# Expert stage of a fused attention and expert kernel: float32r mask, shared V tile for two batches' last tokens, outputs cut at query 256

## Chip, cores and metric

One Trainium2 chip; the kernel runs on 1 core. The metric is the device time of one execution in microseconds, taken as the median over several runs. Before the change it was run 3 times.

## The reference

Three blocks follow each other on 4 batches of 576 tokens, with 512 model columns. First comes an attention with 8 heads whose masks are local (4 heads) or strided (4 heads). Then a mixing layer with cosines, sines and token matrices. Then the block that the change is in, four causal attention experts with a gate that keeps two of them for each token:

```python
def _moe2_ref(x, w_gate, wq, wk, wv, wo):
    logits = x @ w_gate
    topk = np.argpartition(-logits, K, axis=-1)[..., :K]
    ...
    for e in range(E):
        q = x @ wq[e]
        k = x @ wk[e]
        v = x @ wv[e]
        scores = scale * (q @ k.transpose(0, 2, 1))
        scores = np.where(causal, -1000000000.0, scores)
        ...
        ye = a @ v @ wo[e]
        for kk in range(K):
            mask = topk[:, :, kk] == e
            out += mask[..., None] * w[:, :, kk:kk + 1] * ye
```

## The kernel before

Products keep nearly full float32 precision by splitting both sides into a high part in float32r and a low part (the rest). `mm3` (lines 252 to 255) is one such product in three matmuls: high by high, high by low, low by high.

The first 361 us are the sparse attention and the mixing layer; the change leaves their instructions as they are, but for one cast to bf16 at the start (line 73). Behind them the expert stage works batch by batch:

- `project_v` makes V and the gate's logits of a batch: five tiles of tokens, four of 128 and a last one of 64 (`TW`), each with 4 chunks of the model columns by 3 matmuls of 260 columns (256 of V, 4 of the gate). ScalarE casts the result to the high part (line 452), VectorE subtracts to the low part (line 453) and copies the logits (line 454). After the last tile `gates` works out the two best experts with some twenty small VectorE operations.
- `project_qk` makes Q and K of two experts in blocks of 288 tokens (12 matmuls each).
- `attention(b, e, ...)` runs 16 times (4 batches, 4 experts). For each tile t of queries it makes scores against all earlier keys in two matmuls (lines 533, 534), and a third adds the causal mask to the diagonal block: an identity in bf16 is the stationary side, the mask in bf16 the moving one (line 536). The last tile has 64 queries and 576 keys in two chunks of 288, the mask on 64 columns of the second. VectorE takes the maximum, ScalarE the exponential, GpSimd (VectorE for t = 0) scales, TensorE transposes (line 559), ScalarE casts to the high part `pthi` (line 567), VectorE makes the low part `ptlo` (line 568).
- After the loop over t the values are summed in two parts of 288 queries (lines 569 to 589). Key chunk c takes two matmuls, one on `ptlo` (line 579) and one on `pthi` (line 583). The first part has the column counts 288, 160, 32, the second 288, 288, 288, 192, 64, each twice. The result `o` has one PSUM buffer; ScalarE copies half of it (line 588), VectorE adds (line 589).
- `experts` splits the sums of two experts on GpSimd (lines 602, 603) and `output` multiplies by `wo` for one block of 128 model columns (m) and one part of the queries (n): 6 matmuls, a ScalarE copy into a staging slot in X[0] (line 615), and a DMA from SyncE's queue (line 616). There are four slots.

Tiles are recorded in program order and a scheduler that works with a timeline of its own sets the order on each engine; each engine then takes its instructions strictly in that order, and waits on semaphores. The `fill` lists hand projections and outputs of the neighbouring batches to the places in the attention loop from which they may be taken.

## Time and profile before

| what | value |
|---|---|
| median of 3 runs | 582.23 us (581.08 to 583.97) |
| profiled execution, its own time | 579.94 us |
| its span, first to last instruction | 578.2 us |
| TensorE matmul busy | 542.3 us, 94% of the span, 4560 matmuls |
| TensorE weight loads busy | 508.1 us, 88% |
| VectorE busy | 412.3 us, 71% |
| ScalarE busy | 316.2 us, 55% |
| GpSimd busy | 234.3 us, 41% |
| mean granted TensorE clock | 0.968 of full speed |

A busy TensorE here means that one matmul at least is in the pipeline. Matmuls overlap: one of 288 columns is shown as about 0.29 us long, but the next starts 0.13 us later. What a matmul costs is therefore read from the distance between two starts, not from its length.

### The profile page before, as it was taken

How to read it: one execution, taken by the hardware profiler on the slowest of the kernel's cores; microseconds unless marked ns; L12 is line 12 of the kernel's file. 1: busy time of each engine (PE TensorE's matmuls, PEld its weight loads, DVE VectorE, ACT ScalarE, POOL GpSimd, SP SyncE). 2: the span in 40 equal slices, each digit the busy share in tenths (PEclk: the TensorE clock that was granted, in tenths of full speed). 3: DMA queues.
4: the chain of work that ended last, by engine and by line, in shares of the span. 5: the costliest groups of instructions: out<-in, count | busy, mean ns of one | idle time of the engine just before them, and what ended most of it. 6: DMA issues, size and time to landing. Idle time of an engine off the chain costs nothing.

```text
span 578.2 us, 12507 instructions
## 1 busy us (share of the span) xinstructions
PE 542.3 (94%) x4560; PEld 508.1 (88%) x4560; DVE 412.3 (71%) x1205; ACT 316.2 (55%) x882; POOL 234.3 (41%) x314
## 2 busy tenths in 40 slices
PE   6787689899999999999999999899999999999996
PEld 6677579799999999999999999898989899899985
DVE  4896897995687456776255553488987888879882
ACT  5754966533536217254142550287678667866873
POOL 3532383650145211445104460365364534534452
PEclk9957969899999999999999999999999999999999
DMA  9557634221322013110100010100001001100012
GB/s 306 191 166 226 224 123 133 95 69 64 95 86 85 2 32 126 37 38 2 56 1 1 1 57 0 37 2 2 1 12 43 31 1 43 34 9 12 32 42 82
DMA packets 18660, 37.53 MB, mean 65 GB/s; under 512 B 2200, under 2 KB 9544, under 8 KB 18600
## 3 DMA queue, kind: packets, MB, share of 16 engines
q1 hardware_dynamic: 18600, 36.74, 19.6%
q8 instruction: 36, 0.59, 0.4%
q14 instruction: 24, 0.20, 0.1%
HBM read 32.01 MB, written 4.72 MB: 64 GB/s over the span
## 4 chain that ended last, share of the span: by engine, by line
PE 67%; DVE 14%; ACT 9%; DMA 5%; issue 2%; POOL 2%; SPq 0%; ACTq 0%; POOLq 0%; DVEq 0%
PE y L253 6%; PE y L254 6%; PE y L255 6%; PE tp L559 3%; PE th L253 3%; PE th L255 3%; PE th L254 3%; PE g L253 2%; PE g L254 2%; PE s L180 2%; PE g L255 2%; PE pq L253 2%; PE o L583 2%; PE s L533 2%; PE av L231 2%
## 5 line engine op out<-in xcount | busy, mean ns | idle before, releaser
L253 PE MATMUL y<-wtk_hi,zhi 128*128 128x288 f32 x288 | 86.9, 303 | 1.6 <-DVE cs L277 0.6
L254 PE MATMUL y<-wtk_lo,zhi 128*128 128x288 f32 x288 | 85.6, 298 | 1.0 <-POOL wtk_lo L100 1.0
L255 PE MATMUL y<-wtk_hi,zlo 128*128 128x288 f32 x288 | 84.5, 296 | 0.0
L314 POOL TENSOR_TENSOR zlo<-cs,zhi 128x512 fp32r<-128x512 f32 (+1 forms) x40 | 49.5, 1249 | 66.0 <-DVE zhi L311 42.1
L556 POOL TENSOR_SCALAR p<-p,sm,gt 128x256 f32<-128x256 f32 (+1 forms) x64 | 45.2, 709 | 57.2 <-DVE sm L554 38.9
L205 POOL TENSOR_TENSOR p<-p,sm 128x288 f32<-128x288 f32 (+2 forms) x48 | 32.3, 682 | 81.0 <-DVE sm L204 60.1
L549 ACT ACTIVATE p<-s,nm 128x128 f32<-128x128 f32 (+2 forms) x96 | 49.5, 517 | 14.8 <-DVE nm L538 10.0
L253 PEld LDWEIGHTS y<-wtk_hi,zhi 128*128 128x128 f32 x288 | 54.2, 188 | 3.0 <-DVE X L329 1.1
L249 POOL TENSOR_TENSOR x_lo<-X,x_hi 128x576 fp32r<-128x576 f32 x24 | 37.0, 1546 | 45.9 <-DVE x_hi L247 35.9
L254 PEld LDWEIGHTS y<-wtk_lo,zhi 128*128 128x128 f32 x288 | 54.2, 188 | 1.3 <-POOL wtk_lo L100 1.1
L255 PEld LDWEIGHTS y<-wtk_hi,zlo 128*128 128x128 f32 x288 | 53.9, 188 | 0.0
L253 PE MATMUL th<-wth_hi,x_hi 128*128 128x256 f32 (+1 forms) x160 | 50.2, 314 | 2.4 <-DVE cs L277 1.5
L538 DVE TENSOR_REDUCE nm<-s 128x1 f32<-128x128 f32 (+2 forms) x96 | 44.4, 469 | 5.2 <-PE s L536 3.9
L254 PE MATMUL th<-wth_lo,x_hi 128*128 128x256 f32 (+1 forms) x160 | 47.5, 297 | 0.0
L255 PE MATMUL th<-wth_hi,x_lo 128*128 128x256 f32 (+1 forms) x160 | 47.4, 297 | 0.0
L180 PEld LDWEIGHTS s<-k,q 128*108 128x108 f32 (+1 forms) x320 | 41.6, 201 | 6.0 <-issue 4.5
L180 PE MATMUL s<-k,q 128*108 128x54 f32 (+2 forms) x320 | 43.4, 279 | 3.4 <-DMA k<-in_kl 3.3
L253 PE MATMUL pq<-x_hi,wqk_hi 128*128 128x288 f32 x128 | 39.9, 312 | 0.7 <-DVE q L505 0.7
L212 ACT COPY pt<-tp 96x384 f32<-96x384 f32 (+2 forms) x44 | 20.8, 473 | 35.4 <-PE tp L208 35.2
L568 DVE TENSOR_TENSOR ptlo<-tp,pthi 128x128 fp32r<-128x128 f32 (+4 forms) x80 | 38.0, 478 | 2.5 <-ACT pthi L567 1.9
L253 PE MATMUL g<-u_hi,wch_hi 128*128 128x288 f32 x128 | 39.4, 308 | 0.2 <-DVE X L351 0.2
L254 PE MATMUL pq<-x_lo,wqk_hi 128*128 128x288 f32 x128 | 37.9, 296 | 0.0
(156 smaller groups left out, 1732.7 us busy)
## 6 DMA issues: line engine op xcount, KB each, us to landing
X<-in_wtk SPq DMA_DIRECT2D x18, 288.0 KB
q<-in_qs SPq DMA_DIRECT2D x8, 594.0 KB
q<-in_ql SPq DMA_DIRECT2D x8, 576.0 KB
out_t<-X SPq DMA_DIRECT2D x32, 144.0 KB
v<-in_vl SPq DMA_DIRECT2D x24, 144.0 KB
k<-in_kl SPq DMA_DIRECT2D x8, 304.0 KB
k<-in_ks SPq DMA_DIRECT2D x8, 288.0 KB
X<-in_wth SPq DMA_DIRECT2D x4, 512.0 KB
```

The source lines that it names most:

```text
L180: nc.tensor.matmul(s[:rm, i * kw:i * kw + w], qt[:, j0 + i, :], kt[:, k0:k0 + w], start=False, stop=i == n - 1)
L205: nc.gpsimd.tensor_tensor(tiles(p), tiles(p), each(sm), op=ALU.mult)
L212: copy(pt[:kw, :n * rm], tp[:kw, :n * rm])
L249: eng.tensor_tensor(lo, x, f(hi), op=ALU.subtract)
L253: nc.tensor.matmul(ps, ahi, bhi, start=first, stop=False)
L254: nc.tensor.matmul(ps, ahi, blo, start=False, stop=False)
L255: nc.tensor.matmul(ps, alo, bhi, start=False, stop=last)
L314: nc.gpsimd.tensor_tensor(lo, zf, f(hi), op=ALU.subtract)
L538: nc.vector.tensor_reduce(nm[:w, t + ci:t + ci + 1], s[:w, :c1 - c0], axis=AX.X, op=ALU.max, negate=True)
L549: nc.scalar.activation(p[:w, c0:c1], scs[ci][:w, :c1 - c0], AF.Exp, bias=nm[:w, t:t + 1], scale=1.0, accum_out=acc)
L556: eng.tensor_scalar(p[:w, :kn], p[:w, :kn], sm[:w, t:t + 1], gt[:w, t, e:e + 1], op0=ALU.mult, op1=ALU.mult)
L568: nc.vector.tensor_tensor(dst(ptlo), src, f(dst(pthi)), op=ALU.subtract)
```

## The change

The mask and the identity of line 536 become float32r copies, `mask_cr` and `identr`, made once on VectorE at the start of the expert stage; the bf16 identity goes. The last 64 tokens of batch 0 and of batch 1 are gathered into one stationary tile of 128 tokens (`xe_hi`, `xe_lo`: 2 casts on ScalarE and 2 subtractions on VectorE of 128 by 256 elements), so that one set of 12 matmuls makes V of both; the same for batches 2 and 3. The second batch's half waits in SBUF (`v_end`, one ScalarE copy), and is cast and split from there. The values are cut at query 256 in place of 288: the first part, queries 0 to 255, is written inside the loop after tile t = 2, the second, 320 queries, after the loop. Splits and outputs follow the same cut, and a staging slot is now chosen by m and the part, so that block m + 2 shares the slot of block m in the same part. Outputs of earlier batches now run over the parts within each block m; the loop at the very end still runs over the blocks within each part. The other moves of declarations only place tiles in memory.

```diff
 HALF = S // 2
 
+QCUT = [(0, 256), (256, S)]
...
     make_identity(nc, ident)
-    identb = const.tile([128, 128], BF16, name="identb")
-    nc.vector.tensor_copy(identb, ident)
...
     xproj, vs, qks, moved = {}, {}, {}, []
+    identr, mask_cr = (cw.tile([128, 128], F32R, name=name) for name in ("identr", "mask_cr"))
+    nc.vector.tensor_copy(identr, ident)
+    nc.vector.tensor_copy(mask_cr, mask_c)
...
+    v_end = cw.tile([64, 260], F32, name="v_end")
...
+        if b % 2 == 0:
+
+            xe_hi, xe_lo = (cp.tile([128, S], F32R, tag=tag, name=f"xe{tag}_{b}")[:, :512].rearrange(
+                "p (c w) -> p c w", c=4) for tag in ("ohi", "olo"))
+            for i in range(2):
+                x, sl = X[b + i][:, :, 512:S], slice(64 * i, 64 * i + 64)
+                nc.scalar.copy(xe_hi[:, :, sl], x)
+                nc.vector.tensor_tensor(xe_lo[:, :, sl], x, f(xe_hi[:, :, sl]), op=ALU.subtract)
 
         def unit(t):
             w, t0 = TW[t], 128 * t
-            pv = ps2.tile([128, 512], F32, tag="acc", name=f"pv_{b}_{t}")
-            for c in range(4):
-                xhi, xlo = xproj[b][c]
-                mm3(pv[:w, :260], xhi[:, t0:t0 + w], xlo[:, t0:t0 + w], wvg_hi[:, c, :], wvg_lo[:, c, :],
-                    c == 0, c == 3)
+            if t < 4 or b % 2 == 0:
+                pv = ps2.tile([128, 512], F32, tag="acc", name=f"pv_{b}_{t}")
+                for c in range(4):
+                    xhi, xlo = (v[:, t0:t0 + 128] for v in xproj[b][c]) if t < 4 else (xe_hi[:, c, :], xe_lo[:, c, :])
+                    mm3(pv[:, :260], xhi, xlo, wvg_hi[:, c, :], wvg_lo[:, c, :], c == 0, c == 3)
+                if t == 4:
+                    nc.scalar.copy(v_end, pv[64:128, :260])
+            else:
+                pv = v_end
             v = pv[:w, :256].rearrange("p (e d) -> p e d", e=NE)
             nc.scalar.copy(vc[:w, t, :, 0, :], v)
             nc.vector.tensor_tensor(vc[:w, t, :, 1, :], v, f(vc[:w, t, :, 0, :]), op=ALU.subtract)
...
+        def values_of(q0, q1):
+            o = ps2.tile([128, 512], F32, tag="o", bufs=1, name=f"o_{b}_{e}_{q0}")
+            ks_ = [c for c in range(NT) if 128 * c < q1]
+            for c in ks_:
+                a = max(q0, 128 * c)
+                cols = slice(448 * c + a, 448 * c + q1)
+                last = c == ks_[-1]
+
+                def low():
+                    nc.tensor.matmul(o[:64, a - q0:q1 - q0], vc[:, c, e, 0, :], ptlo[:, cols], start=False, stop=False)
+
+                if last:
+                    low()
+                nc.tensor.matmul(o[:, a - q0:q1 - q0], vc[:, c, e].rearrange("p a d -> p (a d)"), pthi[:, cols],
+                                 start=c == 0, stop=last)
+                if not last:
+                    low()
+            tmp = cp.tile([64, S - 256], F32, tag="tmp", name=f"tmp_{b}_{e}_{q0}")
+            nc.scalar.copy(tmp[:, :q1 - q0], o[64:128, :q1 - q0])
+            nc.vector.tensor_tensor(of[pr, q0:q1], o[:64, :q1 - q0], tmp[:, :q1 - q0], op=ALU.add)
...
                 if last:
-                    scored = nc.tensor.matmul(s[:w, t0 - c0:t0 - c0 + w], identb[:, :w], mask_c[:, :w],
+                    scored = nc.tensor.matmul(s[:w, t0 - c0:t0 - c0 + w], identr[:, :w], mask_cr[:, :w],
...
             nc.scalar.copy(dst(pthi), src)
             nc.vector.tensor_tensor(dst(ptlo), src, f(dst(pthi)), op=ALU.subtract)
-        for n in range(2):
-            q0, q1 = HALF * n, HALF * (n + 1)
...
+            if t == 2:
+                values_of(*QCUT[0])
+        values_of(*QCUT[1])
...
             ohi = op.tile([128, S], F32R, tag=tags[0], name=f"ohi_{b}_{m}")
             olo = op.tile([128, S], F32R, tag=tags[1], name=f"olo_{b}_{m}")
             for n in range(2):
-                sl = slice(HALF * n, HALF * (n + 1))
+                sl = slice(*QCUT[n])
                 nc.gpsimd.tensor_scalar(ohi[:, sl], of[:, sl], 1.0, 1.0, op0=ALU.mult, op1=ALU.mult)
                 nc.gpsimd.tensor_tensor(olo[:, sl], of[:, sl], f(ohi[:, sl]), op=ALU.subtract)
...
     def output(b, otp, n, m):
-        sl = slice(HALF * n, HALF * (n + 1))
+        q0, q1 = QCUT[n]
+        sl = slice(q0, q1)
         ms = slice(128 * m, 128 * m + 128)
-        i = 4 * n + m
-        ot = X[0][:, 2 + i % 2, HALF * (i // 2 % 2):HALF * (i // 2 % 2) + HALF]
+        ot = X[0][:, 2 + m % 2, sl]
         po = ps2.tile([128, 512], F32, tag="acc", name=f"po_{b}_{m}_{n}")
         for c in range(2):
-            mm3(po[:, :HALF], wo_hi[:, c, ms], wo_lo[:, c, ms], otp[c][0][:, sl], otp[c][1][:, sl], c == 0, c == 1)
-        nc.scalar.copy(ot, po[:, :HALF])
+            mm3(po[:, :q1 - q0], wo_hi[:, c, ms], wo_lo[:, c, ms], otp[c][0][:, sl], otp[c][1][:, sl], c == 0, c == 1)
+        nc.scalar.copy(ot, po[:, :q1 - q0])
         nc.sync.dma_start(out[b, m, :, sl], ot)
...
     for b in range(B):
-        done = [] if b == 0 else [partial(output, b - 1, otp, n, m) for n in range(2) for m in range(4)]
```

The scheduler's order at three places, before and with the change (names are tile names with their indices; the last number counts tiles).

TensorE, mask of the last tile of batch 3, expert 0 (`s_0_4_1`), before:

```order
L533 MATMUL s_0_4_1_7379<-k_0_0_7066,q_0_0_7064 64x288
L534 MATMUL s_0_4_1_7379<-klow_0_4638,q_0_0_7064 64x288
L536 LDWEIGHTS identb
L536 MATMUL s_0_4_1_7379<-mask_c,identb 64x64
L253 MATMUL pq_1_0_1_7321<-x_3_0_hi,wqk_hi 128x288
L254 MATMUL pq_1_0_1_7321<-x_3_0_lo,wqk_hi 128x288
```

and with the change:

```order
L571 MATMUL s_0_4_1_7354<-k_0_0_7035,q_0_0_7033 64x288
L572 MATMUL s_0_4_1_7354<-klow_0_4640,q_0_0_7033 64x288
L574 MATMUL s_0_4_1_7354<-mask_cr,identr 64x64
L253 MATMUL pq_1_0_1_7288<-x_3_0_hi,wqk_hi 128x288
L254 MATMUL pq_1_0_1_7288<-x_3_0_lo,wqk_hi 128x288
```

The bf16 weight load is gone as an instruction of its own (a float32r matmul brings its own load), and the same projection matmul follows.

VectorE at the start of the stage, from the logits of the fourth V tile to the first split of Q (`q_0_0`), before:

```order
L454 COPY lg_4651<-pv_3_4703 128x4
L453 TENSOR_TENSOR vc_4650<-pv_4_4719,vc_4650 64x4x64
L454 COPY lg_4651<-pv_4_4719 64x4
L469 TENSOR_TENSOR cmp_4736<-lg_4651 128x5x3
L469 TENSOR_TENSOR cmp_4736<-lg_4651 128x5
L473 TENSOR_REDUCE mx_4750<-lg_4651 128x5
L471 TENSOR_TENSOR cnt_4735<-cnt_4735,cmp_4736 128x5x3
L471 TENSOR_TENSOR cnt_4735<-cnt_4735,cmp_4736 128x5
L469 TENSOR_TENSOR cmp_4736<-lg_4651 128x5x2 x2
L471 TENSOR_TENSOR cnt_4735<-cnt_4735,cmp_4736 128x5x2 x2
L505 SCALAR_TENSOR_TENSOR q_0_0_4760<-pq_0_0_0_4764,q_0_0_4760 64x288
```

and with the change:

```order
L471 COPY lg_4654<-pv_3_4712 128x4
L471 COPY lg_5073<-v_end 64x4
L470 TENSOR_TENSOR vc_4653<-pv_4_4728,vc_4653 64x4x64
L471 COPY lg_4654<-pv_4_4728 64x4
L470 TENSOR_TENSOR vc_5072<-v_end,vc_5072 64x4x64
L486 TENSOR_TENSOR cmp_4746<-lg_4654 128x5x3
L486 TENSOR_TENSOR cmp_4746<-lg_4654 128x5
L490 TENSOR_REDUCE mx_4760<-lg_4654 128x5
L488 TENSOR_TENSOR cnt_4745<-cnt_4745,cmp_4746 128x5x3
L488 TENSOR_TENSOR cnt_4745<-cnt_4745,cmp_4746 128x5
L486 TENSOR_TENSOR cmp_4746<-lg_4654 128x5x2
L522 SCALAR_TENSOR_TENSOR q_0_0_4770<-pq_0_0_0_4774,q_0_0_4770 64x288
```

Two operations of batch 1 (`lg` and `vc` from `v_end`) now stand ahead of the gate's comparisons (`cmp`, `cnt`), and three of those have moved behind the split of Q.

TensorE in the last attention of all (batch 3, expert 3), from the transposes of tile 1 on, before:

```order
L559 MATMUL tp_3_2_7797<-ident,p_3_2_7778 128x128 x3
L583 MATMUL o_3_0_7846<-pthi_3_7736,vc_6838 128x288
L559 MATMUL tp_3_3_7813<-ident,p_3_3_7803 128x128 x4
L579 MATMUL o_3_0_7846<-ptlo_3_7737,vc_6838 64x288
L583 MATMUL o_3_0_7846<-pthi_3_7736,vc_6838 128x160
L579 MATMUL o_3_0_7846<-ptlo_3_7737,vc_6838 64x160
L579 MATMUL o_3_0_7846<-ptlo_3_7737,vc_6838 64x32
L583 MATMUL o_3_0_7846<-pthi_3_7736,vc_6838 128x32
L559 MATMUL tp_3_4_7838<-ident,p_3_4_7820 128x64 x5
L583 MATMUL o_3_1_7856<-pthi_3_7736,vc_6838 128x288
L579 MATMUL o_3_1_7856<-ptlo_3_7737,vc_6838 64x288
L583 MATMUL o_3_1_7856<-pthi_3_7736,vc_6838 128x288
```

and with the change:

```order
L597 MATMUL tp_3_2_7758<-ident,p_3_2_7739 128x128 x3
L553 MATMUL o_3_0_7764<-pthi_3_7697,vc_6822 128x256
L549 MATMUL o_3_0_7764<-ptlo_3_7698,vc_6822 64x256
L549 MATMUL o_3_0_7764<-ptlo_3_7698,vc_6822 64x128
L553 MATMUL o_3_0_7764<-pthi_3_7697,vc_6822 128x128
L597 MATMUL tp_3_3_7782<-ident,p_3_3_7772 128x128 x4
L597 MATMUL tp_3_4_7807<-ident,p_3_4_7789 128x64 x5
L253 MATMUL po_0_0_7835<-ohi_1_7829,wo_hi 128x256
L553 MATMUL o_3_256_7815<-pthi_3_7697,vc_6822 128x320
L253 MATMUL po_1_0_7844<-ohi_1_7829,wo_hi 128x256
L254 MATMUL po_0_0_7835<-olo_1_7830,wo_hi 128x256
L255 MATMUL po_0_0_7835<-ohi_1_7829,wo_lo 128x256
```

The first part (`o_3_0`) has moved ahead of the transposes of tile 3 and lost its narrowest pair, and output matmuls (`po`) of the first part now stand between the transposes of tile 4 and the second part (`o_3_256`).

## Rows read from the trace of the kernel before

**Rows 1.** Page, span in 40 slices: granted TensorE clock in tenths of full speed

```profile
PEclk9957969899999999999999999999999999999999
```

**Rows 2.** Busy time by stretch: span us, then PE, PEld, DVE, ACT, POOL; clock, DMA

```profile
372.00:400.00 28.00, 26.12 (x197) 23.45 (x196) 25.06 (x87) 20.72 (x62) 14.50 (x24) 1.00 0.01 2
...
400.00:560.00 160.00, 158.56 (x1229) 144.25 (x1229) 135.60 (x483) 115.34 (x349) 73.97 (x127) 1.00 0.07 24
520.00:560.00 40.00, 40.00 (x316) 36.68 (x315) 35.16 (x121) 30.32 (x94) 18.39 (x33) 1.00 0.09 31
```

**Rows 3.** Longest waits of TensorE (PE) and its loads (PEld), 400 to 560 us

```profile
PE po L253 <- ACT X L615: 0.4, 1, 0.4
...
PEld L536 <- issue: 7.5, 35, 0.3
```

**Rows 4.** Timeline of PE around a mask of a last tile: start, length, instruction

```profile
465.05 0.29 PE L534 MATMUL s<-klow,q 128*64 128x288 f32 x1
465.28 0.22 PE L536 MATMUL s<-mask_c,identb 128*64 128x64 bf16 x1
465.42 0.40 PE L253 MATMUL pq<-x_hi,wqk_hi 128*128 128x288 f32 x1
465.66 0.29 PE L254 MATMUL pq<-x_lo,wqk_hi 128*128 128x288 f32 x1
```

**Rows 5.** Timeline of PE around a mask of a full tile, then a matmul

```profile
510.85 0.23 PE L536 MATMUL s<-mask_c,identb 128*128 128x128 bf16 x1
510.89 0.48 PE L533 MATMUL s<-k,q 128*128 128x512 f32 x1
511.21 0.40 PE L534 MATMUL s<-klow,q 128*128 128x512 f32 x1
511.44 0.23 PE L536 MATMUL s<-mask_c,identb 128*128 128x128 bf16 x1
```

**Rows 6.** Timeline of PE, a mask of a full tile, then four transposes

```profile
485.83 0.23 PE L536 MATMUL s<-mask_c,identb 128*128 128x128 bf16 x1
485.90 0.61 PE L559 MATMUL tp<-ident,p 128*128 128x128 f32 x4
```

**Rows 7.** Timeline of PE, float32r matmuls of 128 by 128 on 128 columns

```profile
475.20 0.31 PE L533 MATMUL s<-k,q 128*128 128x128 f32 x1
475.34 0.28 PE L534 MATMUL s<-klow,q 128*128 128x128 f32 x1
```

**Rows 8.** Weight loads: bf16 (tile identb, ns min/median/max), float32r (group, mean ns)

```profile
L536 PEld LDWEIGHTS <-identb x80: 94/96/107, 377.7 to 560.6; 128*128 128x128 bf16 x64, 128*64 128x64 bf16 x16
...
L533 PEld LDWEIGHTS s<-k,q 128*128 128x128 f32 x64 | 12.0, 192 | 1.0 <-POOL k L510 0.5
```

**Rows 9.** Timeline of PE, two matmuls of V

```profile
366.50 0.29 PE L253 MATMUL pv<-wvg_hi,x_hi 128*128 128x260 f32 x1
366.62 0.29 PE L254 MATMUL pv<-wvg_lo,x_hi 128*128 128x260 f32 x1
```

**Rows 10.** Timeline of PE, last matmul of a first part, and the next

```profile
436.81 0.26 PE L583 MATMUL o<-pthi,vc 128*128 128x32 f32 x1
436.93 0.33 PE L533 MATMUL s<-k,q 128*64 128x288 f32 x1
```

**Rows 11.** Group of VectorE, low part of V: mean ns of one

```profile
L453 DVE TENSOR_TENSOR vc<-pv,vc 128x256 fp32r<-128x256 f32 x12 | 5.0, 419 | 2.1 <-ACT vc L452 1.9
```

**Rows 12.** Waits of PE, 372 to 400 us and 560 us to the end

```profile
PE pq L253 <- DVE q L505: 0.7, 1, 0.7
...
PE o L583 <- ACT pthi L567: 0.7, 1, 0.7
```

**Rows 13.** End: last copy (ACT), output DMAs' issue (ns min/median/max), SyncE's last wait

```profile
574.93 0.40 ACT L615 COPY X<-po 128x288 f32<-128x288 f32 x1 [0.40 <-PE po L255]
...
L616 SPq DMA_DIRECT2D out_t<-X x32: 332/332/431, 432.3 to 575.4; - x32
...
SPq L722 <- DMA out_t<-X: 1.4, 1, 1.4
```

More of the change, by code (lines that the diff above doesn't have):

```diff
@@ L49, in fused_kernel, with new_mask @@
     xpool = ctx.enter_context(tc.tile_pool(name="xpool", bufs=1))
-    def new_mask(name, shape):
-        t = const.tile(shape, BF16, name=name)
+    X = [xpool.tile([128, 4, S], F32, name=f"X{b}") for b in range(B)]
+    act = ctx.enter_context(tc.tile_pool(name="act", bufs=4))
+    ph1 = ctx.enter_context(ExitStack())
+    wb = ph1.enter_context(tc.tile_pool(name="wb", bufs=1))
+    def new_mask(name, shape, pool):
+        t = pool.tile(shape, BF16, name=name)
         nc.gpsimd.memset(t, 0.0)
@@ L59, in select @@
                                 base=base, channel_multiplier=cm)
-    mask_l = new_mask("mask_l", [128, 4, LK])
+    mask_l = new_mask("mask_l", [128, 4, LK], wb)
     select(mask_l[:64, 1, :], [[1, LK]], -1, -1)
@@ L71, in fused_kernel @@
     make_identity(nc, ident)
-    identb = const.tile([128, 128], BF16, name="identb")
-    nc.vector.tensor_copy(identb, ident)
     twice = []
     for rw in (LQ, RQ):
-        t = const.tile([128, 2, rw], BF16, name=f"twice{rw}")
+        t = wb.tile([128, 2, rw], BF16, name=f"twice{rw}")
         nc.vector.tensor_copy(t, ident[:, None, :rw].to_broadcast([128, 2, rw]))
         twice.append(t.rearrange("p a c -> p (a c)"))
-    mask_s = new_mask("mask_s", [128, 5, RQ])
+    mask_s = new_mask("mask_s", [128, 5, RQ], wb)
     select(mask_s[:64, 0, :], [[-1, RQ]], 0, 1)
@@ L85, in fused_kernel @@
     nc.vector.memset(mask_s[:64, 4, 2 * BLK:], MASKED / SCALE)
-    mask_c = new_mask("mask_c", [128, 128])
+    mask_c = new_mask("mask_c", [128, 128], const)
     select(mask_c, [[-1, 128]], 0, 1, MASKED)
-    X = [xpool.tile([128, 4, S], F32, name=f"X{b}") for b in range(B)]
-    act = ctx.enter_context(tc.tile_pool(name="act", bufs=4))
-    ph1 = ctx.enter_context(ExitStack())
-    wb = ph1.enter_context(tc.tile_pool(name="wb", bufs=1))
     pha = ph1.enter_context(ExitStack())
@@ L568, in attention @@
             nc.vector.tensor_tensor(dst(ptlo), src, f(dst(pthi)), op=ALU.subtract)
-        for n in range(2):
-            q0, q1 = HALF * n, HALF * (n + 1)
-            o = ps2.tile([128, 512], F32, tag="o", bufs=1, name=f"o_{b}_{e}_{n}")
-            ks_ = [c for c in range(NT) if 128 * c < q1]
-            for c in ks_:
-                a = max(q0, 128 * c)
-                cols = slice(448 * c + a, 448 * c + q1)
-                last = c == ks_[-1]
-                def low():
-                    nc.tensor.matmul(o[:64, a - q0:HALF], vc[:, c, e, 0, :], ptlo[:, cols], start=False, stop=False)
-                if last:
-                    low()
-                nc.tensor.matmul(o[:, a - q0:HALF], vc[:, c, e].rearrange("p a d -> p (a d)"), pthi[:, cols],
-                                 start=c == 0, stop=last)
-                if not last:
-                    low()
-            tmp = cp.tile([64, HALF], F32, tag="tmp", name=f"tmp_{b}_{e}_{n}")
-            nc.scalar.copy(tmp, o[64:128, :HALF])
-            nc.vector.tensor_tensor(of[pr, q0:q1], o[:64, :HALF], tmp, op=ALU.add)
+            if t == 2:
+                values_of(*QCUT[0])
+        values_of(*QCUT[1])
     def experts(b, fill):
@@ L651, in fused_kernel @@
     for b in range(B):
-        done = [] if b == 0 else [partial(output, b - 1, otp, n, m) for n in range(2) for m in range(4)]
+        done = [] if b == 0 else [partial(output, b - 1, otp, n, m) for m in range(4) for n in range(2)]
         fill = [x + y + z for x, y, z in zip(
```

## The prediction, before the changed kernel ran

> **What bounds the kernel now.** I began with the page's slices of the span. The granted clock is at full speed (the 2.4 GHz level) from the middle of the span to its end [rows 1], so no part of the expert stage, which is all that the change touches, can gain from the clock. Next, busy time by stretch [rows 2]: from 400 to 560 us TensorE is busy 158.6 of 160 us. In the first stretch of the attentions, 372 to 400 us, it is busy 26.1 of 28 and VectorE 25.1 of 28: there both are near their limit. After 560 us TensorE waits for single steps of others [rows 12]: a chain, then the last outputs. The waits agree [rows 3]: between 400 and 560 us the longest wait of the matmuls is 0.4 us in total. The weight loads of the bf16 mask alone stand idle for 7.5 us "issue", 35 times, with nothing to wait for. So in 160 us the order of things is: whatever TensorE need not do is time, as long as nothing else takes over.
>
> What a matmul takes is the distance between two starts. A plain float32r matmul of 288 columns has 0.13 us, of 512 columns 0.23 us (511.21 to 511.44 in [rows 5]), of 260 columns 0.12 us [rows 9].
>
> **V of two batches.** Four last tiles of 12 matmuls become two: 24 matmuls by 0.12 us [rows 9] = **-2.9 us** of TensorE. A stationary tile of 128 instead of 64 tokens costs nothing more, since [rows 9] is already one of 128. Added are four casts on ScalarE and four subtractions on VectorE of 128x256, 0.42 us each on VectorE by [rows 11], and two copies of `v_end`. Half of them, and the two casts of identity and mask, stand before 372 us, where TensorE makes the first four V tiles and the others have little to do; the other half is covered by VectorE's spare time, 24 of 160 us from 400 to 560 us [rows 2]. Without that cover they would cost 0.8 us.
>
> **Mask.** Before a last tile's mask [rows 4]: from the second score matmul (465.05) to the second matmul behind the mask (465.66) it is 0.61 us, where two plain steps would be 0.26, so this mask takes 0.35 us. Before a full tile's [rows 5]: mask to next 0.04 us, but the next matmul then takes 0.32 where a plain one of its size takes 0.23, so 0.13 us. With transposes behind it [rows 6] 0.07 us. In the program 51 of the 64 full masks have a matmul behind them and 13 a transpose: 51 x 0.13 + 13 x 0.07 + 16 x 0.35 = 13.1 us. In float32r no row shows it. Lower end: 128 columns at the pace of the 512, 0.06 us, which makes 80 of them 4.8 us (-8.3). Upper end: score matmuls of the same shape [rows 7], 0.14 us, 11.2 us (-1.9). I take the 0.11 us of the transposes (0.61 less one length of 0.28, over three steps, [rows 6]), also float32 with 128 stationary columns and 128 moving ones: 8.8 us, **-4.3 us**.
>
> A bf16 load takes 0.096 us, a float32r load 0.192 [rows 8], and the change trades the first for the second. The Trainium skill ("TensorE: Matmul & The Clock Gate", Weight-path perf modes) says that weights load fast where there are 128 of them and the type is not FP32; by it the mask on full tiles would become dearer, not cheaper. The rows show loads of 0.192 us behind matmuls that start every 0.13 us, so loads are hidden in the stream. That they are not stays a rival, below.
>
> **Cut at 256.** The columns per attention stay the same, 3,200; two matmuls go. The narrowest pair, 2 x 32 columns, takes 0.12 us for its second matmul alone [rows 10], where 64 columns at the plain pace are 0.03 us. Some of it will remain with the pair of 128 columns that is now last: -0.1 us in 16 attentions = **-1.6 us** (ends 0 and, for 0.12 each, -1.9).
>
> **What of this does not count.** About two of the 16 attentions run before 400 us with VectorE as busy as TensorE, and the last one is a chain in which TensorE waits: 3/16 of mask and cut is lost, **+1.1 us**. At the start VectorE has a copy and a subtraction of batch 1 (0.56 us) ahead of the gate and of the split of Q, as the order above shows; a Q projection waits for that split already (0.7 us, [rows 12]): **+0.5 us** (ends 0 and 1.0, as part of the gate moved behind it). From 372 to 560 us VectorE is busy 161 us (25.1 and 135.6) and gets 1 more, while TensorE's time falls by 7 to 8 of 188: 90% busy, where the highest share beside a full TensorE is 88% (35.2 of 40, [rows 2]). For that I take **+0.8 us** (ends 0 and 3).
>
> **The end.** Six output matmuls move ahead of the second part, and 36 instead of 42 follow it: about -1.0 us. But block m = 2 now shares the slot of m = 0, two outputs earlier instead of four. A slot's round is a copy of 0.40 us, its DMA's issue of 0.33 us and 1.4 us until it has landed [rows 13], 2.1 us and more, while two outputs of 320 columns take 2 x 6 x 0.15 = 1.8 us, and those of m = 0 and 1 end close together because their matmuls are interleaved. The last copies will wait: +0.5 us. Together **-0.5 us** (ends -1.0 and +0.3). The Trainium skill ("DMA: Bandwidth & Descriptors", Anatomy of one DMA) gives a fixed cost of about 2.0 us per DMA, mostly the wait for the write's receipt; by its figure the round is about 0.3 us longer and the end gains 0.2 us.
>
> Sum: -2.9 -4.3 -1.6 +1.1 +0.5 +0.8 -0.5 = **-6.9 us**. The profiled execution took 579.94 us and would take 573.0. It lies 2.3 us below the median of the runs, 582.23, so on the runs' scale I forecast **575.3 us**.
>
> **Rivals.**
> - *VectorE takes over.* If it cannot be busier than the 88% seen beside a full TensorE, 372 to 560 us shrinks to 162/0.88 = 184 us, a gain of 4.4; with start and end about -4.4: 577.8. For it: 25.1 of 28 us in the first stretch, where TensorE falls behind. Against: that same 90%, and 88% in the last batch without any wait of TensorE.
> - *All of it and more.* The mask runs at the pace of its columns (-8.3 instead of -4.3; of the further 4.0 us 3/16 don't count, 3.3 remain), VectorE keeps up (0.8): -11.0, 571.3. For it: nothing in a stream of one type seems to wait for loads. Against: [rows 7].
> - *The mask gets dearer.* If a load's longer time came through, 64 masks would take 0.096 us more and 16 about 0.03: +6.6 instead of -4.3, in all -2.9 +6.6 -1.6 = +2.1, 584.3. Against: the hidden loads. The Trainium skill's rule on fast weight loads, cited above, points this way.
> - *Slower: the first part blocks TensorE's queue.* It now stands in the loop, close behind the transposes whose cast and low part it needs, and TensorE takes its instructions in order. In the last attention a part like that waited 0.7 us for `pthi` [rows 12]. If all 16 do so, 11.2 us come on top: +4.3, 586.5. It decides against the change from 0.6 us per attention, (6.9 + 2.9)/16. Against: the scheduler puts other matmuls between in most places, and in 400 to 560 us it left 0.4 us of such waits.
>
> **Chances.** A measurement tells about 0.5% (2.9 us) from no change. Forecast 0.52, VectorE 0.18, more 0.11, all three below 579.3: faster 0.81. Mask dearer 0.11: same. Queue blocked 0.08: slower. The range goes down to the rival with more, 571.0, and up past VectorE's (577.8, with start and end at their bad ends 579.1) by the 0.25% that the runs before scatter: 580.5. Left out are the last two, 0.19.
>
> **What would show it.** Right: 24 matmuls of V on the last tiles instead of 48; mask rows in float32r, with a step of 0.11 us to the next and no step of 0.3 behind it; no "issue" wait of a mask's load; TensorE still busy 99% from 400 us on, VectorE 88% to 90%. Wrong: waits of TensorE for `ptlo`, `pthi` or `nm` of more than 2 us between 390 and 550 us (VectorE or the queue), a score group that is no shorter than before (mask). At the end a wait of ScalarE's copies for the output's DMA of about half a microsecond is expected.

## The result and the profile after

The changed kernel takes **574.94 us** (median of four runs, 573.85 to 576.09) where the kernel before, run beside it, took 583.1: a ratio of 0.985 (95% interval 0.982 to 0.988). In a second comparison it took 576.66 us (six runs, 574.49 to 578.07) and the kernel before 580.88: 0.992 (0.990 to 0.994). Over all runs of this study the medians are 575.95 us (10 runs) and 581.5 us (80 runs, which scatter from 577.5 to 587.2): 5.5 us or just under 1% faster.

For the place of the gain each profile is cut at marks that every version has: the first matmul of V, the first mask, the last mask and the end of the span. First and last start stand in the rows of the mask and of V in the view by line (here with ns min/median/max, then first and last start in us). Of the changed kernel:

```profile
L574 PE MATMUL s<-mask_cr,identr x80: 191/222/278, 376.0 to 553.7; 128*128 128x128 f32 x64, 128*64 128x64 f32 x16
...
L253 PE MATMUL pv<-wvg_hi,x_hi x64: 278/283/387, 359.9 to 508.7; 128*128 128x260 f32 x64
...
L253 PE MATMUL pv<-wvg_hi,xeohi x8: 281/282/367, 366.5 to 460.8; 128*128 128x260 f32 x8
```

and of the kernel before:

```profile
L536 PE MATMUL s<-mask_c,identb x80: 216/230/234, 377.7 to 560.6; 128*128 128x128 bf16 x64, 128*64 128x64 bf16 x16
...
L253 PE MATMUL pv<-wvg_hi,x_hi x80: 277/283/386, 362.1 to 514.7; 128*128 128x260 f32 x64, 128*64 128x260 f32 x16
```

With the spans, 578.17 and 572.58 us, this pair divides its 5.6 us so: 2.2 us before the first matmul of V, where the change does nothing; +0.6 us from there to the first mask; **-5.3 us** in the attentions, first mask to last; +1.3 us behind the last mask. Of V's 80 matmuls of this kind 16 on 64 tokens have become 8 on the shared tile; `mm3` has three kinds, so 24 are gone, as forecast.

TensorE's own steps came out as forecast. A full tile, then a last tile with a mask, in PE's timeline of the changed kernel, which answer to [rows 5] and [rows 4]:

```profile
483.51 0.33 PE L572 MATMUL s<-klow,q 128*128 128x384 f32 x1
483.68 0.22 PE L574 MATMUL s<-mask_cr,identr 128*128 128x128 f32 x1
483.74 0.44 PE L571 MATMUL s<-k,q 128*128 128x512 f32 x1
484.02 0.39 PE L572 MATMUL s<-klow,q 128*128 128x512 f32 x1
...
501.74 0.29 PE L572 MATMUL s<-klow,q 128*64 128x288 f32 x1
501.87 0.19 PE L574 MATMUL s<-mask_cr,identr 128*64 128x64 f32 x1
501.90 0.36 PE L253 MATMUL pv<-wvg_hi,x_hi 128*128 128x260 f32 x1
502.10 0.28 PE L254 MATMUL pv<-wvg_lo,x_hi 128*128 128x260 f32 x1
```

Mask to next is 0.06 us, and the 512 columns behind it take 0.28 instead of 0.23: 0.11 us for the mask. On the last tile 0.03, and 0.20 instead of 0.12: again 0.11, where [rows 4] gave 0.35. By the same reckoning over all masks the median is 0.11 us for the 57 full and the 13 last-tile masks with a matmul behind them (0.12 and 0.34 before), but 0.20 for the 7 full ones with a transpose behind them (0.13 before); the 3 last-tile masks with a transpose behind them cost nothing more (0.29 before). By these medians the 80 masks fall from 13.3 us to 9.0, 4.3 less.

But TensorE is no longer full. Busy time by stretch of the changed kernel, the first two rows to be read against [rows 2], and its longest waits from 400 to 560 us, against [rows 3] (waited for: us in total, times, longest):

```profile
372.00:400.00 28.00, 25.44 (x189) 24.02 (x190) 24.86 (x83) 19.83 (x59) 15.30 (x24) 1.00 0.00 1
400.00:560.00 160.00, 155.94 (x1207) 148.16 (x1206) 139.32 (x500) 120.16 (x364) 76.96 (x132) 1.00 0.07 24
...
400.00:553.70 153.70, 151.45 (x1174) 144.59 (x1174) 135.03 (x484) 115.82 (x352) 73.77 (x126) 1.00 0.07 25
```

```profile
PE o L553 <- DVE sm L592: 1.2, 1, 1.2
PE s L571 <- ACT p L587: 1.1, 3, 0.5
PE po L253 <- ACT X L635: 0.6, 2, 0.3
PE po L253 <- POOL ohi L622: 0.5, 1, 0.5
```

Between 400 and 560 us it stands idle for 4.1 us, before for 1.4. But the last mask now stands at 553.7 us, so this stretch takes in 6 us of the end, and the waits for `sm` and for GpSimd's `ohi` lie there. Up to the last mask it is idle 2.2 of 153.7 us (third row), in the kernel before 1.4 of 160.6:

```profile
400.00:560.60 160.60, 159.16 (x1232) 144.57 (x1231) 136.16 (x486) 115.92 (x350) 74.02 (x128) 1.00 0.07 23
```

The mask's loads no longer have a row of "issue" there. Between 372 and 400 us a wait of V's matmuls for the low part of batch 1's X has become the longest, 0.5 us before (the row here) and 2.1 now (rows in the section on the mask taken out, below).

```profile
PE pv L255 <- DVE x_lo L249: 0.5, 1, 0.5
```

At the end ScalarE's copies of the outputs, in ScalarE's timeline (the bracket is the idle time ahead and what ended it):

```profile
560.93 0.65 ACT L635 COPY X<-po 128x256 f32<-128x256 f32 x2 [1.40 <-PE po L255]
...
564.21 0.67 ACT L635 COPY X<-po 128x256 f32<-128x256 f32 x2 [1.56 <-DMA out_t<-X]
...
568.77 0.89 ACT L635 COPY X<-po 128x320 f32<-128x320 f32 x2 [1.60 <-DMA out_t<-X]
```

Two of them wait 1.6 us each for the DMA that still reads their place, and behind the first TensorE waits too (its next output matmul has the bracket 0.96 us for ScalarE's `X`).

### The profile page after: what moved, and what is told of

Read it like the earlier page. It is cut to its first block, busy times and chain, and to the rows that moved or that the text cites. A ratio compares the mean times of both kernels' runs of the same rounds, so it can differ in the third digit from the quotient of the medians.

```text
span 572.6 us, 12429 instructions
## 1 busy us (share of the span) xinstructions
PE 536.2 (94%) x4504; PEld 510.2 (89%) x4504; DVE 415.4 (73%) x1210; ACT 317.8 (55%) x888; POOL 236.2 (41%) x314
## 4 chain that ended last, share of the span: by engine, by line
PE 64%; DVE 17%; ACT 11%; DMA 3%; issue 3%; POOL 1%; SPq 0%; ACTq 0%; POOLq 0%; DVEq 0%
PE y L253 6%; PE y L254 6%; PE y L255 6%; PE s L180 4%; PE th L253 3%; PE th L255 3%; PE tp L597 3%; PE th L254 3%; PE g L253 2%; PE g L254 2%; PE av L231 2%; PE g L255 2%; DVE nm L576 2%; PE tp L208 2%; PE s L571 2%
## 5 line engine op out<-in xcount | busy, mean ns | idle before, releaser
L249 POOL TENSOR_TENSOR x_lo<-X,x_hi 128x576 fp32r<-128x576 f32 x24 | 38.5, 1609 | 44.5 <-DVE x_hi L247 34.9
L253 PE MATMUL th<-wth_hi,x_hi 128*128 128x256 f32 (+1 forms) x160 | 48.6, 304 | 3.2 <-DVE cs L277 2.3
L180 PEld LDWEIGHTS s<-k,q 128*108 128x108 f32 (+1 forms) x320 | 43.5, 209 | 4.4 <-issue 4.3
L180 PE MATMUL s<-k,q 128*108 128x54 f32 (+2 forms) x320 | 45.3, 288 | 1.9 <-DMA k<-in_kl 1.9
L255 PE MATMUL th<-wth_hi,x_lo 128*128 128x256 f32 (+1 forms) x160 | 46.1, 289 | 0.0
L254 PE MATMUL th<-wth_lo,x_hi 128*128 128x256 f32 (+1 forms) x160 | 46.1, 288 | 0.0
```

The costliest lines, as they stand in the source:

```text
L180: nc.tensor.matmul(s[:rm, i * kw:i * kw + w], qt[:, j0 + i, :], kt[:, k0:k0 + w], start=False, stop=i == n - 1)
L249: eng.tensor_tensor(lo, x, f(hi), op=ALU.subtract)
L253: nc.tensor.matmul(ps, ahi, bhi, start=first, stop=False)
L254: nc.tensor.matmul(ps, ahi, blo, start=False, stop=False)
L255: nc.tensor.matmul(ps, alo, bhi, start=False, stop=last)
```

## The experiments

Theories. **Stage:** the effect is TensorE's saved time in the expert stage, less new waits at named places (low part of X, end). **Placement or scatter:** part of it lies in the first 360 us. **VectorE:** it shares the bound, and so part of what TensorE saves does not arrive. All runs in one table; "runs" is the median less that of the kernel before in the same comparison, with the interval of the ratio; the other columns are from one profile each, in us:

| version | runs | ratio, 95% | first V | to first mask | attentions | TensorE idle in them | last mask to end |
|---|---|---|---|---|---|---|---|
| before | | | 362.1 | 15.6 | 182.9 | 2.7 | 17.6 |
| changed (first) | -8.2 | 0.982 to 0.988 | 359.8 | 16.2 | 177.7 | 4.6 | 18.9 |
| changed (again) | -4.2 | 0.990 to 0.994 | 362.7 | 16.2 | 177.7 | 4.5 | 18.3 |
| places only | +0.1 | 0.997 to 1.002 | 362.6 | 15.6 | 184.5 * | | 18.9 * |
| mask only | -1.9 | 0.993 to 0.999 | 360.2 | 15.6 | 182.2 | 4.7 | 17.4 |
| V only | -4.1 | 0.990 to 0.995 | 360.0 | 16.2 | 179.9 | 2.6 | 18.9 * |
| cut only | -1.3 | 0.994 to 0.999 | 362.9 | 15.6 | 182.1 | 3.2 | 17.8 |
| changed, bf16 mask | -5.1 | 0.987 to 0.994 | 361.0 | 16.1 | 177.7 | 2.4 | 19.2 * |
| changed, own slots | -6.2 | 0.987 to 0.992 | 360.0 | 16.2 | 178.9 * | | 17.5 |
| changed, low parts on VectorE | -0.2 | 0.998 to 1.002 | 359.8 | 16.2 | 181.5 | | 19.7 * |
| changed, 80 copies more | +3.6 | 1.004 to 1.008 | 363.3 | 16.2 | 184.9 * | 9.3 | 18.2 |
| changed, 80 additions fewer | -7.5 | 0.984 to 0.992 | 362.8 | 16.2 | 176.7 | 3.7 | 20.2 * |
| before, 80 additions fewer | -2.1 | 0.994 to 1.001 | 361.0 | 15.6 | 183.1 * | | 18.7 * |
| 80 fewer and own slots | -7.6 | 0.982 to 0.990 | 364.1 | 16.2 | 176.7 | | 17.2 |

A star marks a part in which TensorE ran at its lower clock for a short while; what that costs is shown first. The scheduler orders each version anew. Compared by name and shape between first and last mask, TensorE's order is unchanged in places only (from before) and in own slots (from the change); with the bf16 mask some 60 of 1336 matmuls stand elsewhere, with the 80 copies about 190, and in the versions with one part alone, with the low parts on VectorE or with fewer additions 40% to 70%. What those differ by holds their new order too.

### Places only

```
-    def new_mask(name, shape):
-        t = const.tile(shape, BF16, name=name)
+    def new_mask(name, shape, pool):
+        t = pool.tile(shape, BF16, name=name)
...
-        t = const.tile([128, 2, rw], BF16, name=f"twice{rw}")
+        t = wb.tile([128, 2, rw], BF16, name=f"twice{rw}")
```

> The kernel before with the pools moved as in the change (two masks and the doubled identities in the pool that is closed ahead of the expert stage, X and the activation pool opened first), and nothing else; every engine's instructions stand in the same order. In the profiled pair 2.24 us of the 5.58 us between the spans lay ahead of the first V matmul (359.85 against 362.09 us). Theory 'stage' (the whole effect is TensorE's in the expert stage, the earlier difference is scatter of the start): no change, within 1 us of before. Rival 'placement' (where the tiles lie decides something in the first 360 us): about -2.2 us, all of it ahead of the first V matmul.

Measured: +0.1 us, no effect. The first V matmul came at 362.6 us, and at 362.7 us in the changed kernel's second profile: over the fourteen profiles it lies between 359.8 and 364.1 us in no order that follows the version. The 2.2 us of the first pair are scatter. Yet with the same order of instructions the attentions took 1.5 us longer than before. The busy time by stretch of this version shows why (after the five engines' busy time comes the granted clock):

```profile
391.00:395.00 4.00, 2.78 (x20) 2.06 (x18) 3.97 (x10) 3.57 (x11) 2.75 (x5) 1.00 0.00 0
...
396.00:398.00 2.00, 2.00 (x11) 1.97 (x11) 1.40 (x7) 0.40 (x1) 1.10 (x2) 0.50 0.00 0
```

Right behind a stretch in which TensorE was busy 2.78 of 4 us its clock fell to half, the 1.2 GHz level, for 3 to 4 us. In the kernel before it was as idle there, and the clock stayed at 1.00:

```profile
391.00:395.00 4.00, 2.78 (x18) 1.86 (x17) 3.97 (x11) 3.41 (x10) 2.67 (x6) 1.00 0.00 0
395.00:398.00 3.00, 3.00 (x25) 2.89 (x26) 2.81 (x15) 1.77 (x7) 1.72 (x3) 1.00 0.00 0
```

Where two versions have the same order, one such fall costs 1.2 to 1.6 us (184.5 against 182.9, and 18.9 against 17.6 at the end; the version with own slots 178.9 against 177.7). Part of the runs' scatter is probably this: only one execution of each version has a trace, but over 75 runs of the kernel before with a clock on record (the longest left out) the longer ones have the lower mean clock (correlation -0.46). Single profiles are compared here by their undisturbed parts.

### One part alone

Each is the kernel before with the places moved and one part of the change. Mask:

```
-                    scored = nc.tensor.matmul(s[:w, t0 - c0:t0 - c0 + w], identb[:, :w], mask_c[:, :w],
+                    scored = nc.tensor.matmul(s[:w, t0 - c0:t0 - c0 + w], identr[:, :w], mask_cr[:, :w],
```

> The kernel before with the pools moved and the mask in float32r; V, the cut and the outputs as before. Theory 'stage': 80 masks cost about 0.11 us instead of 0.16 on average, -4.2 us of TensorE's steps, of which 3.5 to 4.2 us arrive, since VectorE has no more work than before. Rival 'placement': the same and 2.2 us more, about -6. Rival 'nothing hidden comes free' (VectorE is the bound beside TensorE): under -1.5 us.

V:

```
+            if t < 4 or b % 2 == 0:
...
+                if t == 4:
+                    nc.scalar.copy(v_end, pv[64:128, :260])
+            else:
+                pv = v_end
```

> The kernel before with the pools moved and V of two batches' last tokens in one tile; mask, cut and outputs as before. 24 matmuls fewer: -2.7 us of TensorE's steps. Against it stand the first tile of the stage, which now waits for 128 tokens' casts and subtractions (about +0.8 us between the first V matmul and the first mask in the changed kernel), and a wait for batch 1's low part between 372 and 400 us (2.1 us there, 0.5 before). Theory 'stage, start dear': -0.5 to -1.5 us. Rival 'start cheap' (these waits come from the mask or the cut): -2.2 us or more.

Cut:

```
+            if t == 2:
+                values_of(*QCUT[0])
+        values_of(*QCUT[1])
```

> The kernel before with the pools moved and the parts of 256 and 320 queries, the first inside the loop, outputs by block; mask and V as before. TensorE's steps: -1.1 us over 16 attentions. At the end six output matmuls (about 1.0 us) move ahead of the second part, but the copies wait 3.2 us for the slots' DMAs as in the changed kernel. Theory: -0.5 to -1.5 us, and the stretch from the last attention's last matmul to the end of the span no shorter than before. Rival 'queue blocked': the first part waits in TensorE's queue, slower by 1 us or more.

Measured, in the profiles: V alone makes the attentions 3.0 us shorter for 2.9 us of TensorE's busy time, all of it; the cut 0.8 us for 1.3. The mask alone makes them 0.8 us shorter, although TensorE is busy 2.75 us less. First mask to last mask of mask only, of V only and of the cut only (TensorE's busy time is the first after the length, VectorE's the third):

```profile
375.86:558.04 182.18, 177.52 (x1392) 168.94 (x1391) 155.11 (x554) 134.00 (x404) 88.26 (x147) 1.00 0.06 21
```

```profile
376.25:556.16 179.91, 177.35 (x1369) 160.38 (x1368) 157.31 (x554) 135.00 (x407) 90.24 (x147) 1.00 0.06 21
```

```profile
378.49:560.59 182.10, 178.94 (x1362) 160.92 (x1361) 155.61 (x555) 134.80 (x405) 88.13 (x147) 1.00 0.06 21
```

The mask's saved time has become idle time: 4.7 us instead of 2.7. It stands in the waits of mask only from 372 us on (1.0 us of the first row and 0.3 of the last lie behind the last mask):

```profile
PE o L581 <- DVE X L587: 2.0, 3, 1.0
PE s L531 <- ACT p L547: 1.0, 3, 0.4
PE tp L557 <- DVE sm L551: 1.0, 2, 0.6
PE po L248 <- ACT X L613: 0.8, 3, 0.3
```

The chains through VectorE and ScalarE now end later than TensorE needs them. In the runs the three give -1.9, -4.1 and -1.3 us, each with some 1.5 us of uncertainty. For the mask the 3.5 to 4.2 us of 'stage' did not come; the profile is near the rival 'nothing hidden comes free'. "Start dear" was right in its place (first mask 0.6 us later with V alone), but V's gain was above the range given for it and in that of 'start cheap'. The cut came as expected, and the first part did not block the queue.

### The mask taken out of the change

```
-                    scored = nc.tensor.matmul(s[:w, t0 - c0:t0 - c0 + w], identr[:, :w], mask_cr[:, :w],
+                    scored = nc.tensor.matmul(s[:w, t0 - c0:t0 - c0 + w], identb[:, :w], mask_c[:, :w],
```

> The changed kernel with the mask in bf16 as before; V, the cut and the outputs as in the change. In the steps of TensorE the mask's change is worth 4.4 us here and 4.2 us in the kernel before, where alone it made the stretch from the first V matmul to the last matmul only 0.84 us shorter (new gaps of 0.2 to 0.7 us between matmuls took 3.5 us), while V alone gave 2.5 and the cut 1.0, nearly all of their steps. Theory 'the mask's saved time does not arrive' (score tiles end earlier, but the next step waits for VectorE and ScalarE all the same): +0.5 to +1.5 us against the changed kernel. Rival 'the order' (the scheduler drew up a poor order for the mask alone; in the changed kernel's order it arrives): +3 to +4.5 us.

Measured: 575.96 us, -5.1 against the kernel before, where the changed kernel had -4.2; the attentions take 177.65 us in both. First mask to last mask with the bf16 mask, then of the changed kernel's second profile:

```profile
377.11:554.76 177.65, 175.27 (x1337) 158.43 (x1337) 155.35 (x554) 135.27 (x407) 87.96 (x146) 1.00 0.06 21
```

```profile
378.90:556.55 177.65, 173.12 (x1338) 165.01 (x1337) 156.84 (x553) 134.01 (x407) 87.92 (x146) 1.00 0.06 21
```

TensorE is busy 2.15 us less with the float32r mask and idle 2.15 us more. (By its steps the mask saves 4.3; a gap that is shorter than the overlap of two matmuls does not show as idle time.) So over the attentions the mask's term is nil in these profiles, just under the range of 'does not arrive', and the rival 'the order' (+3 to +4.5) fell. The runs fit that, -5.1 against -5.5 over all runs of the change, with some 2 us of uncertainty. The parts do not simply add: V alone and the cut alone give 3.8 us of the attentions together, both without the mask 5.3 (182.9 to 177.65); where the rest comes from is not shown.

Nil is the sum of a loss and a gain. As the two orders are nearly the same, the way can be divided at the 29th of the 80 masks. First mask to 29th and 29th to last, with the bf16 mask, then with the change:

```profile
377.11:430.98 53.87, 52.41 (x395) 46.29 (x395) 48.49 (x181) 41.89 (x127) 29.84 (x50) 1.00 0.01 4
430.98:554.76 123.78, 122.85 (x944) 112.14 (x944) 106.86 (x374) 93.38 (x280) 58.12 (x97) 1.00 0.09 29
```

```profile
378.90:434.51 55.61, 52.18 (x394) 48.69 (x394) 50.41 (x181) 41.47 (x127) 29.71 (x50) 1.00 0.01 4
434.51:556.55 122.04, 120.94 (x945) 116.32 (x943) 106.43 (x374) 92.54 (x280) 58.21 (x97) 1.00 0.09 30
```

The first stretch is 1.74 us longer with the float32r mask, and TensorE is idle there for 3.4 us instead of 1.5; the second is 1.74 us shorter, nearly all of the 1.9 us by which TensorE is less busy in it. (The first profile of the change has the same lengths within 0.02 us.) So behind the 29th mask, with VectorE 87% busy, the mask's time arrives; before it, with VectorE 91% busy and V of batch 1 to be made, it is lost and as much again. The waits from 372 to 560 us, bf16 mask and changed kernel:

```profile
PE o L552 <- DVE sm L591: 1.2, 1, 1.2
PE pv L257 <- POOL x_lo L251: 0.9, 2, 0.5
PE s L570 <- ACT p L586: 0.7, 2, 0.5
```

```profile
PE pv L255 <- DVE x_lo L249: 2.1, 2, 1.1
PE s L571 <- ACT p L587: 1.1, 3, 0.5
PE pq L253 <- DVE q L522: 0.8, 2, 0.7
PE po L253 <- ACT X L635: 0.6, 2, 0.3
```

The wait for the low part is 1.2 us longer, that for the exponentials 0.4, that for the copies 0.2 (the wait for `sm` lies behind the last mask in both). The first, and all but a little of the second, lie in the first stretch. With the bf16 mask VectorE's two low parts take 0.76 and 0.98 us, and the first is done when GpSimd's first begins; with the change GpSimd's begin first, and VectorE's take 1.52 and 1.41 (next section). With the bf16 mask:

```profile
L251 DVE TENSOR_TENSOR x_lo<-X,x_hi x2: 760/871/982, 388.3 to 390.6; 128x576 fp32r<-128x576 f32 x2
```

### The low part of batch 1

```
-        eng = nc.vector if len(xsplit) == B and name.endswith(("0", "2")) else nc.gpsimd
+        eng = nc.vector if len(xsplit) == B and ("_1_" in name or name.endswith(("0", "2"))) else nc.gpsimd
```

> The changed kernel; all four low parts of batch 1's X are made on VectorE, where two of them were made on GpSimd. In the changed kernel the two on VectorE took 1.52 and 1.41 us, each beside one of GpSimd's (1.41 us), where one with GpSimd idle took 0.73 in the kernel before; V's matmuls waited 2.1 us for them. Theory 'the two engines slow each other': four by 0.7 to 0.9 us, the wait of V's matmuls for the low part falls under 0.8 us, -0.8 to -1.5 us in all. Rival 'VectorE is full there': the wait moves to the split of Q and K or to the maximum, no gain, or up to 1.5 us slower.

Measured: the four on VectorE take 0.74 us each and the wait falls from 2.1 to 0.7 us, as the theory had it; but in all the version is 4 us slower than the changed kernel, more than the rival had, with longer waits elsewhere (for ScalarE's exponentials 2.0 us, for `pthi` 1.5). As half of TensorE's matmuls stand in another place, it does not say what the wait alone is worth. The changed kernel's timelines of GpSimd and of VectorE:

```profile
387.82 1.41 POOL L249 TENSOR_TENSOR x_lo<-X,x_hi 128x576 fp32r<-128x576 f32 x1 [0.73 <-ACT x_hi L245]
...
390.22 1.41 POOL L249 TENSOR_TENSOR x_lo<-X,x_hi 128x576 fp32r<-128x576 f32 x1
```

```profile
388.32 1.52 DVE L249 TENSOR_TENSOR x_lo<-X,x_hi 128x576 fp32r<-128x576 f32 x1
...
390.83 1.41 DVE L249 TENSOR_TENSOR x_lo<-X,x_hi 128x576 fp32r<-128x576 f32 x1
```

and the version with all four on VectorE, by line:

```profile
L249 DVE TENSOR_TENSOR x_lo<-X,x_hi x4: 740/740/740, 388.3 to 391.7; 128x576 fp32r<-128x576 f32 x4
```

These subtractions on VectorE, which begin 0.5 and 0.6 us behind those on GpSimd, take twice as long. The Trainium skill ("SBUF — State Buffer", Who interferes with whom) says that an instruction of VectorE with two inputs in SBUF contends with one of GpSimd that reads SBUF, that the ports they share are locked by one of them at a time, and that the order of issue decides which one waits. As an estimate by that rule the first would end at 387.82 + 1.41 + 0.74 = 389.97 us and the second at 392.37; the rows have 389.84 and 392.24, so the trace agrees within 0.13 us.

### VectorE's load, more and less

```
             nc.vector.reciprocal(sm[:w, t:t + 1], sm[:w, t:t + 1])
+            nc.vector.tensor_copy(extra[:w], sm[:w, t:t + 1])
```

> The changed kernel with 80 small copies on VectorE (128x1 of the reciprocal, one per tile of scores, read by nobody), 0.13 to 0.15 us each by the rows of such operations, about 11 us of VectorE in the 190 us of the attentions, which takes it from 88% to some 94% busy. Theory 'local waits' (VectorE has room, and TensorE waits only at a few places): 0 to +2.5 us. Rival 'VectorE is the bound beside TensorE, and this is why only half of TensorE's saved time arrives': +6 us or more.

```
-            nc.vector.tensor_scalar_add(sm[:w, t:t + 1], sm[:w, t:t + 1], 1e-9)
```

> The changed kernel without the addition of 1e-9 to the sums of the exponentials (80 operations of VectorE, 0.14 us each by the rows, 11.3 us; each sum is at least 1, where float32 does not take in 1e-9). The 80 added copies on VectorE made the stage some 5 us longer. Theory 'VectorE shares the bound' (about two thirds of VectorE's time comes through beside a full TensorE): the reverse, -3 to -6 us against the changed kernel, the waits of V's matmuls for the low part and of the scores for ScalarE's exponentials fall. Rival 'adding hurts, removing does not help' (TensorE is the bound from here on): -1 us or less.

> The kernel before without the same 80 additions. Theory 'VectorE shares the bound': in the kernel before TensorE's steps are 8.2 us longer and cover VectorE better, so they gain less than in the changed kernel, -0.5 to -2.5 us, and the change is worth 6 to 8 us between the two kernels without the additions, where it was worth 4 to 5 with them. Rival 'the lost time is not VectorE's' (order of the scheduler, places): the same gain as in the changed kernel, and the change is worth 4 to 5 us as before.

Measured: with the 80 copies 584.43 us, 7.8 us above the changed kernel beside it. First mask to last mask of this version, and of the one with 80 additions fewer:

```profile
379.47:564.34 184.87, 175.61 (x1338) 166.08 (x1337) 164.26 (x631) 134.38 (x407) 88.95 (x146) 0.99 0.06 21
```

```profile
378.98:555.63 176.65, 172.92 (x1337) 164.22 (x1337) 149.44 (x477) 134.65 (x407) 89.51 (x146) 1.00 0.06 22
```

VectorE 7.4 us busier makes the attentions 7.2 us longer, some 1.5 of it a fall of the clock (0.59 from 452 to 455 us): three quarters come through. 'Local waits' fell; the rival's 6 us or more came. VectorE 7.4 us less busy makes them 1.0 us shorter, as 'adding hurts, removing does not help' had it: the cover is used up on the one side, and on the other something else holds. In the kernel before the same 80 additions were worth 2.1 us in the runs, about 1.0 to 1.4 in the attentions (183.1 with one fall of the clock). Between the two versions without them the change is worth 5.4 us in the runs, between the two ranges given, and about 5 in the attentions, 5.3 with them. That VectorE's throughput alone takes the mask's time is thus not borne out, as far as versions with such different orders can tell.

### The end

```
-        ot = X[0][:, 2 + m % 2, sl]
+        ot = X[1][:, m, sl] if b == B - 1 else X[0][:, 2 + m % 2, sl]
```

> The changed kernel once more, unchanged, beside the kernel before: the four runs so far give a median of 574.94 us, and the start of a run scatters by some 3 us. Theory 'stage': between 574 and 577 us, 4.5 to 7 us under before; from the first V matmul to the last matmul again 208.75 us (212.47 before), within 0.3 us as long as the granted clock stays at full speed there.

> The changed kernel; the last batch's outputs are written from the tile X of batch 1, free by then, so that each of the eight has a place of its own. The order of the instructions stays the same. Theory (the end is held by the slots: two copies of ScalarE wait 1.6 us each for a DMA, and TensorE stands 1.24 and 0.53 us behind them): no such wait, -1.2 to -1.8 us, from the last attention's last matmul to the end of the span. Rival (the low parts of the last part on GpSimd or the DMAs themselves hold the end): under 0.5 us.

Measured: the changed kernel once more has its attentions within 0.03 us of the first profile, and its end 0.6 us shorter; from the first V matmul to the last matmul 208.2 us, 0.6 under the first profile, where 0.3 had been allowed. Against the kernel beside it it gains 4.2 us, just short of the 4.5 expected. With slots of their own 574.72 us against 576.66 for the changed kernel on the same chip, 1.9 us. The copies wait for TensorE alone; in ScalarE's timeline of this version:

```profile
565.14 0.37 ACT L635 COPY X<-po 128x256 f32<-128x256 f32 x1 [0.33 <-PE po L255]
566.75 0.75 ACT L635 COPY X<-po 128x320 f32<-128x320 f32 x2 [1.24 <-PE po L255]
568.41 0.42 ACT L635 COPY X<-po 128x320 f32<-128x320 f32 x1 [0.91 <-PE po L255]
```

From the last mask to the end are 17.5 us, where the changed kernel has 18.3 and 18.9: 0.8 to 1.4 us, about the lower end of the theory's range. It is now as long as before, not shorter.

### Both together

> The changed kernel without the 80 additions and with a place of its own for each of the last eight outputs. Theory: both effects add, as one acts in the attentions and the other at the end: 2 us (the measured effect of the places) under the version without the additions, 4 to 8 us under the changed kernel.

Measured: 574.66 us, 0.986 (0.982 to 0.990) of the kernel before. In the profile, first V matmul to end, 210.1 us, where the changed kernel has 212.7 and 212.1, and the kernel before 216.1: the best version found, 2.0 to 2.7 us under the changed kernel there. In the runs (572.4 to 576.3, six) it is not told apart from it with certainty, and the 4 us or more that were expected did not come.

## Why the forecast came out, and what in it did not

The forecast of 575.3 us held, in part by chance: its sum is 1.4 us more than the gain over all runs, and its terms hold only in part.

- **What bounds it** (full TensorE, so "whatever TensorE need not do is time, as long as nothing else takes over"). This step failed at the condition. TensorE's busy time between first and last mask fell by 7.15 us (180.27 to 173.12), the attentions by 5.3.
- **V**, -2.9: right. Alone: 2.9 us of busy time, 3.0 in the attentions. The casts and subtractions were covered.
- **Mask**, -4.3: the price of 0.11 us was right, the arrival was not. Alone it brings 0.8 us in the attentions, within the change 0.0: 1.7 us lost up to the 29th mask, 1.7 gained behind it. The place of the loss was named (VectorE as busy as TensorE before 400 us), its size was not: three sixteenths of the saving were taken off, when what is lost there, most of it behind a later low part, equals what the rest brings. Of the rivals, *all of it and more* and *the mask gets dearer* fell: the first needs 0.06 us a mask, the second would have made TensorE busier, and the rows have 0.11 us beside loads of 189 ns.
- **Cut**, -1.6: about half, 0.8 us in the attentions for 1.3 of busy time. *The first part blocks the queue* fell.
- **Start**, +0.5: 0.6 measured, but not by the wait that was named. The one for the split of Q is 0.7 us before and after; the stretch from the first Q matmul to the first mask grows by 0.5 us elsewhere. The number is right in part by luck.
- **VectorE**, +0.8: too small. The gain of the rival *VectorE takes over* (4.4, though its own 188 - 184 us make 4) is near to what the profiles show, 3.4 and 4.0 us from the first V matmul to the end. Its limit of 88% is not borne out: with the mask alone VectorE is 85.1% busy in the attentions and TensorE's time is lost all the same, with 80 copies more it is 88.9%, with 80 additions fewer 84.6% and the gain is 1.0. The wait that was named nowhere is the one for the low part of X, 2.1 us.
- **End**, -0.5: failed. It is 0.7 to 1.3 us longer. The wait for the place of an output was foreseen as +0.5; it was 1.6 us, twice, of which 0.8 to 1.4 reach the end. The -1.0 for six output matmuls that move ahead isn't seen even without that wait (17.5 against 17.6): the last attention is a chain (TensorE waits 1.2 us for `sm`), and what is moved into it shortens no link.
- **The sum**, -6.9 from the profiled execution: the profiles' undisturbed parts give -3.4 and -4.0, the runs -8.2, -4.2 and over all -5.5. The profiled execution of before, 579.94 us, had no fall of the clock in the expert stage and is 1.5 us shorter than the median of all its runs. That the change also makes such falls rarer would close the rest. The mean granted clock points that way, 0.962 over the same 75 runs of before and 0.965 over the ten of the change, where one fall is worth 0.003; but it takes in the first 360 us as well, so it is not shown.

Open stays whether the loss in the first stretch comes from the shorter masks themselves or from the some 60 matmuls that stand elsewhere: the same order with either mask was not tried, as the order is not given by hand. Shown is where it lies, that 1.2 us of it are the wait for the low parts, which VectorE makes more slowly behind GpSimd's, and that behind it the saved time arrives. Why the mask alone brings only 0.8 us, in an order of its own, stays open too.

## What to carry to other kernels

An engine that is busy 99% is not yet a bound that pays back what is taken from it: look whether a second one is near 90% on the same chains, stretch by stretch, and price the term by a run that changes it alone. Here V's matmuls paid in full. The mask's time arrived where VectorE was 87% busy and was lost, with as much again, where it was 91% busy and a low part came late. A sum of nil can be a gain and a loss: follow two versions of nearly the same order mark by mark. Where an output's place is used again, count copy, issue and landing against the time to the next use, with the outputs bunched as they really end. Cut single profiles at marks within the program before comparing them, waits included: a stretch fixed in microseconds took 6 us of the end into the changed kernel's idle time.

## What the runs showed of the chip

Two things were not expected. TensorE's clock fell to half within the expert stage in eight of fourteen profiles (the ten stars above), in one run and not in another of the same order of instructions; where it was looked at, behind a stretch of waits. A fall cost 1.2 to 1.6 us, as much as a term of the sum. And a subtraction of VectorE on 128x576 took 0.74 us alone and 1.41 to 1.52 behind one of GpSimd, on the path of TensorE.
